# Score products on contiguous key chunks, and values loaded in 256-byte pieces, one pair of heads at a time

## The chip, the cores and the metric

The kernel runs on one NeuronCore of a Trainium2 chip. The metric is the device time of one execution in microseconds (us). The engines are PE (TensorE matmul; PEld is its weight load), DVE (VectorE), ACT (ScalarE), POOL (GpSimd) and SP (SyncE), which here only issues transfers.

## The reference

```python
def rmsnorm(x, g): return x / np.sqrt(np.mean(x * x, -1, keepdims=True) + 1e-06) * g
q_n, k_n = rmsnorm(q, g_q), rmsnorm(k, g_k)
scores = (1 / np.sqrt(64)) * q_n @ k_n.transpose(0, 1, 3, 2)
attn = softmax(scores)                     # over the keys
x = (attn @ v) -> (3584 tokens, 768)       # q, k, v: (8, 12, 448, 64) float32
e = argmax(x @ w_gate + modality_bias[modality_id], 1)      # one of 8 experts
out[t] = gate[t] * relu(x[t] @ w1[e]) @ w2[e]               # w1 768x1024, w2 1024x768
```

Eight batches of twelve heads go through attention over 448 keys of 64 values each; every token of the result then goes through one of eight experts.

## The kernel before, in words

The program has two stages. The first is attention, the second the experts, in blocks of 256 tokens. The change touches the first alone.

**Units and chunks.** Attention goes over 48 units (`NU`); a unit is two heads of one batch. The 2 x 448 keys of a unit are cut into seven chunks of 128, j = 0 to 6. Chunks 0 to 2 hold 384 keys of head 0, chunks 4 to 6 those of head 1, and chunk 3 the 64 keys left of each head. A unit takes seven steps, one a chunk; n = 7 u + j counts them.

**What PE does in a step.** `st` (L844) makes the scores of one chunk, keys on the partitions and 448 queries along the row: one matmul with a high part of the keys (`kkf`, 128 rows, in `w1w`) and one with a low part (`khf`, 65 rows, in `w2ha` or `w1w`). The keys are the stationary operand, so each matmul first loads 128 columns of them. `columns` (L805) says which. In chunk 3 the columns are contiguous, and there are four matmuls, since the heads need one pair each. In the six others the columns lie three apart: chunk j takes every third key from j % 4 on. ACT makes `p`, the exponentials of the scores. `sa` (L812) makes scores once more with queries on the partitions, two units ahead, for the row maxima that DVE takes; its stationary operand is contiguous. Beside these two a step holds at most a few other groups, placed by the numbers of `PLAN` (L34): `tr` (transposing a later unit's normalised keys, step 0, and queries, step 3), `av` (L883, values times `p` of the unit before, steps 1, 4 and 6), `mt` (step 1), `xt` (step 4), `sums` (step 2 of every second unit), `gates` and `recips` (`sp`, step 2 of every fourth unit). So of the six strided chunks five follow such a small group on PE, and chunk 6 follows a `sa`.

**Transfers.** SP issues them in program order. In each unit there are eight `move`s (L764: high and low parts of keys and queries to other partitions, 64 rows of 1,792 bytes), a row of maxima (L839), and the loads of q and k of a later unit (L677). After every third unit comes the store of finished columns (L963) and then `load_v` (L659), which loads the values of three units at once by four transfers. The keys of a chunk lie three apart so that a partition's three values are neighbours in DRAM: `(p j)` gives 768-byte pieces. The order of `move`s matters to PE: those of `tr` of the queries (step 3, at -18) are needed by the first `sa` (at -14) four steps later, those of the keys (at -21) seven steps later.

Of the kernel before, what the change touches and what calls it, by code (L numbers as in the profile page):

```python
# [18 lines left out]
B, H, S, D = 8, 12, 448, 64  # L19
# [3 lines left out]
NP = H // 2  # L23
NU = B * NP
# [42 lines left out]
def kernel(  # L67
# [16 lines left out]
    PE, SY = nc.tensor, nc.sync  # L84
# [52 lines left out]
    def load_gate():  # L137
        with nc.allow_non_contiguous_dma(reason="small gate tables"):
            for half in range(2):
                SY.dma_start(wg[64 * half : 64 * half + 64, :, 8 * half : 8 * half + 8],  # L140
                             w_gate.rearrange("(j h p) e -> h p j e", h=2, p=64)[half])
            SY.dma_start(modr, mod_id.bitcast(I32).rearrange("(b p w) -> p b w", b=B, p=CP))
        SY.dma_start(
            bia.rearrange("p m e -> p (m e)"),
            mod_bias.rearrange("m e -> (m e)").unsqueeze(0).to_broadcast([CP, 2 * NE]),
        )
# [205 lines left out]
    def view(t, off, p, *dims):  # L352
        n = 1
        for d in dims:
            n *= d
        a = t[:p, off : off + n]
        if len(dims) > 1:
            ax = " ".join("abcd"[: len(dims)])
            a = a.rearrange(f"p ({ax}) -> p {ax}", **dict(zip("abcd"[1:], dims[1:])))
        return a  # L360
# [14 lines left out]
    def two(t):  # L375
        return [t[:, 0:S], t[:, S + 64 : WZ]]
# [8 lines left out]
    p_b, v_b = ([view(t, o, 128, *sh) for t in (r2w, at_l)]  # L385
                for o, sh in ((0, (NJ, S)), (PW, (3, NJ, D))))
# [40 lines left out]
    def wload(s, which, halves=(0, 1)):  # L427
        tb, i = tb_of(s)
        raw, src = ((r1, w1v), (r2, w2v))[which]
        for h in halves:  # L430
            G.indirect_dma_start(out=raw[h], out_offset=None, in_=src,
                                 in_offset=IOFF(ap=tb["wi"][:, i, h : h + 1], axis=0),
                                 bounds_check=NE * 256 - 1, oob_is_err=False)
# [212 lines left out]
    if True:  # L646
# [7 lines left out]
        HB = {}  # L654
# [1 line left out]
        X = {}  # L656
        R = {}

        def load_v(hb):  # L659
            b, h0 = hb // 2, 6 * (hb % 2)  # L660
            t = HB.setdefault(hb, {})
            t["v"] = v_b[hb % 2]

            for h in range(2):
                src = v[b, h0 : h0 + 6].rearrange("(u h) s d -> h u s d", h=2)[h]
                SY.dma_start(t["v"][:, :, 4 * h : 4 * h + 3].rearrange("p u j d -> p u (j d)"),
                             src[:, 64 * h : 64 * h + 384].rearrange("u (p j) d -> p u (j d)", j=3))
                SY.dma_start(t["v"][64 * h : 64 * h + 64, :, 3],
                             src[:, 384 * (1 - h) : 384 * (1 - h) + 64].rearrange("u p d -> p u d"))


        def load(u):
            b, h0 = u // NP, 2 * (u % NP)
# [131 lines left out]
        def columns(t, j):  # L805

            if j == 3:
                return [(h, t[:, 384 + 64 * h : 512 + 64 * h]) for h in range(2)]
            h = j // 4
            return [(h, two(t)[h][:, bass.ds(64 * h + j % 4, 128, step=3)])]  # L810

        def sa(u, j):  # L812
            t = T[u]
# [30 lines left out]
        def st(u, j):  # L844
            t = T[u]
            if j == 0:
                t["p"] = p_b[u % 2]
            ps = ps_s.tile([128, 512], F32, tag="s", name=f"st{u}_{j}")
            for first in (True, False):
                for h, l in columns(t["kkf" if first else "khf"], j):  # L850
                    PE.matmul(ps[:, :S], lhsT=l, rhs=t["qq"][:, h] if first else t["ql"][:, h],  # L851
                              start=first and (j != 3 or h == 0), stop=not first and (j != 3 or h == 1))

            def act():
                A.activation(out=t["p"][:, j], in_=ps[:, :S], func=AF.Exp)

            return act
# [310 lines left out]
        for n in range(P["start"], NJ * NU):  # L1168
            i, j = divmod(n, NJ)
# [56 lines left out]
            if 0 <= i < NU and j in CSJ:  # L1226
                h = CSJ.index(j)
# [12 lines left out]
            if done and len(routed) < B - 1 and done[-1] >= (NP * len(routed) + 5) // 4:  # L1240
                b = len(routed)
# [7 lines left out]
                    slow.append(("exp", tables1))  # L1249
            if n == -4:  # L1250
                load_v(0)
                load_gate()
                SY.dma_start(l_d.rearrange("(p r) w -> p (r w)", p=128), zt)
            for h in range(2):
# [10 lines left out]
            if i == NU - 1:  # L1265
                for m in sorted(fin):
                    run(fin, m)
                wload(0, 1)
            if (i + 1) % 3 == 0 and 0 < (i + 1) // 3 < 2 * B:
                load_v((i + 1) // 3)  # L1270

        after = []

# [11 lines left out]
        u, g = NU - 1, NU // 4 - 1  # L1285
# [43 lines left out]
        for s in range(NSTAT):  # L1329
# [34 lines left out]
            for b_ in range(16):  # L1364
                t, j = divmod(b_, 8)
# [79 lines left out]
```

## Time and profile before

| | us |
|---|---|
| median of 3 runs | 1141.43 |
| lowest and highest | 1140.6, 1145.1 |
| the profiled execution | 1139.65 |
| its span, first to last instruction | 1137.9 |
| PE busy | 1089.8 (96%) |
| PE weight loads busy | 856.9 (75%) |
| DVE busy | 863.7 (76%) |
| ACT busy | 827.7 (73%) |
| POOL busy | 656.8 (58%) |

Matmuls are pipelined on PE and their ends are modelled, so its busy time says when it had work, not how fast that went; the distance from the start of one matmul to the start of the next says more. A matmul's weight load can run under the matmul before it.

### The profile page before, as it was taken

The page shows a single profiled execution, that of the slowest core. Times are in us where ns is not written, and L with a number is a line of the kernel's source. Part 1 is how long each engine was busy: PE and PEld are TensorE (multiplying, and loading weights), DVE is VectorE, ACT ScalarE, POOL GpSimd, SP SyncE. Part 2 cuts the span into 40 slices and gives each one's busy share as a digit, 9 for nine tenths or more (in the row PEclk, how much of TensorE's full clock was granted, in tenths as well). Part 3 has the DMA queues.
Part 4 walks back from the last instruction along what each step waited for, and adds up shares of the span by engine and source line. Part 5 has one row for each costly group of instructions (what it writes and reads, how often), then busy time and mean ns, then how long its engine had stood idle before and what let it go on. Part 6 is the DMA issues. An engine that isn't in the chain of part 4 may idle for free. (4 is left out here: it accounts for less than half of the span.)

```text
span 1137.9 us, 19896 instructions
## 1 busy us (share of the span) xinstructions
PE 1089.8 (96%) x6678; PEld 856.9 (75%) x6678; DVE 863.7 (76%) x1598; ACT 827.7 (73%) x1605; POOL 656.8 (58%) x665
## 2 busy tenths in 40 slices
PE   7899999999999999999999999999999999999993
PEld 6655655566565565555568899999999999999981
DVE  4676778988779988789688987767777677776770
ACT  6878888778787787775666677668776687766770
POOL 4577677777777787777764565444244433345430
PEclk8899999999999999999999999999999999999996
DMA  7656567666576666665725111111161111111360
GB/s 170 169 127 154 127 174 173 167 161 148 141 180 162 163 144 160 168 147 114 212 66 189 26 46 59 40 57 56 43 252 41 56 43 56 32 40 56 115 186 11
DMA packets 101345, 131.78 MB, mean 116 GB/s; under 512 B 29979, under 2 KB 95983, under 8 KB 99696
## 3 DMA queue, kind: packets, MB, share of 16 engines
q1 hardware_dynamic: 83588, 88.57, 32.0%
q0 software_dynamic: 17616, 41.80, 11.7%
q8 instruction: 57, 0.93, 0.4%
q14 instruction: 56, 0.46, 0.1%
q10 hardware_dynamic: 28, 0.01, 0.0%
HBM read 148.74 MB, written 22.38 MB: 150 GB/s over the span
## 5 line engine op out<-in xcount | busy, mean ns | idle before, releaser
L485 PE MATMUL ph<-xw,w1w 128*128 128x256 f32 x2016 | 246.1, 283 | 1.8 <-DVE hlw L52 1.0
L485 PEld LDWEIGHTS ph<-xw,w1w 128*128 128x128 f32 x2016 | 243.9, 192 | 3.8 <-issue 1.4
L52 DVE TENSOR_REDUCE at_hlw<-sa 128x1 f32<-128x448 f32 x336 | 206.9, 618 | 48.3 <-PE sa L823 30.0
L52 DVE TENSOR_TENSOR w1w<-r,w1w 128x256 fp32r<-128x256 f32 x360 | 221.0, 672 | 13.8 <-ACT w1w L52 13.5
L52 ACT CAST w1w<-r 128x256 fp32r<-128x256 f32 x360 | 224.8, 722 | 0.0
L851 PE MATMUL st<-w1w 128*128 128x448 f32 (+1 forms) x480 | 191.7, 448 | 1.1 <-ACT r2w L52 0.8
L851 PEld LDWEIGHTS st<-w1w 128*128 128x128 f32 (+1 forms) x480 | 107.3, 239 | 45.1 <-ACT r2w L52 21.2
L52 ACT ACTIVATE hhw<-ph 128x512 fp32r<-128x512 f32 x56 | 33.5, 598 | 121.8 <-PE ph L485 121.8
L52 POOL TENSOR_TENSOR r2w<-r2w 128x448 f32<-128x448 f32 (+1 forms) x72 | 82.4, 1144 | 68.4 <-DVE r2w L52 30.6
L52 ACT ACTIVATE r2w<-st 128x448 f32<-128x448 f32 x168 | 90.0, 541 | 40.7 <-PE st L851 35.7
L823 PE MATMUL sa<-w1w 128*128 128x448 f32 (+1 forms) x288 | 110.6, 385 | 8.9 <-DVE at_hlw L52 5.8
L515 PE MATMUL py<-w2lw,hhw 128*128 128x384 f32 x448 | 113.9, 335 | 0.0
L851 PE MATMUL st<-w1w,w2ha 65*128 65x448 f32 x288 | 102.5, 376 | 3.1 <-DMA r2w<-in_v_dram 2.5
L52 ACT ACTIVATE at_w2lw<-st 128x448 f32<-128x448 f32 x168 | 89.3, 540 | 13.4 <-PE st L851 11.6
L52 POOL TENSOR_TENSOR xrw<-r,at_hlw 112x512 f32<-112x512 f32 x95 | 97.4, 1045 | 2.5 <-PE tr L752 2.2
L52 POOL DMA_INDIRECT out_dram<-yw,lb_oi x22 | 28.3, 1286 | 122.0 <-ACT yw L52 118.9
L515 PEld LDWEIGHTS py<-w2lw,hhw 128*128 128x128 f32 x448 | 80.9, 188 | 0.0
L52 DVE SCALAR_TENSOR_TENSOR hlw<-ph,hhw 128x512 fp32r<-128x512 f32 x56 | 38.7, 691 | 51.9 <-ACT hhw L52 51.9
L52 ACT ACTIVATE w1w<-tr,gs 64x448 fp32r<-64x448 f32 x96 | 60.3, 629 | 23.0 <-DVE xw L52 22.3
L52 POOL TENSOR_TENSOR r2w<-r2w,at_w2lw 64x448 f32<-64x448 f32 (+1 forms) x48 | 54.9, 1144 | 38.0 <-DVE r2w L52 19.5
L851 PEld LDWEIGHTS st<-w1w,w2ha 65*128 65x128 f32 x288 | 70.9, 246 | 5.4 <-DMA r2w<-in_v_dram 2.7
L52 ACT ACTIVATE xrw<-r 112x512 f32<-112x512 f32 (+1 forms) x124 | 64.6, 526 | 9.7 <-DMA r<-in_k_dram 7.2
(297 smaller groups left out, 2297.9 us busy)
## 6 DMA issues: line engine op xcount, KB each, us to landing
w1w<-xw SPq DMA_DIRECT2D x312, 112.0 KB
r<-in_q_dram SPq DMA_DIRECT2D x48, 224.0 KB
r<-in_k_dram SPq DMA_DIRECT2D x48, 224.0 KB
w2ha<-xw SPq DMA_DIRECT2D x72, 112.0 KB
x_d<-at_w2hb SPq DMA_DIRECT2D x8, 672.0 KB
x_d<-yw SPq DMA_DIRECT2D x8, 672.0 KB
r2w<-in_v_dram SPq DMA_DIRECT2D x16, 288.0 KB
at_w2lw<-in_v_dram SPq DMA_DIRECT2D x16, 288.0 KB
```

The lines of the kernel that those rows point to most:

```text
L52: return fn(*a, **kw)
L485: PE.matmul(ps[:, i], lhsT=lt_, rhs=rt_[:, c], start=n == 0, stop=n == 17)
L515: PE.matmul(ps[n][:, :384], lhsT=lt_[:, j, 128 * t : 128 * t + 128], rhs=rt_[:, 384 * n : 384 * n + 384], start=j == 0 and m == 0, stop=j ...
L823: PE.matmul(ps[:, :S], lhsT=t["qq"][r, h, a : a + 128], rhs=t["kk"][h][r], start=True, stop=True)
L851: PE.matmul(ps[:, :S], lhsT=l, rhs=t["qq"][:, h] if first else t["ql"][:, h], start=first and (j != 3 or h == 0), stop=not first and (j != ...
```

## The change

Chunk j of a head now takes 128 neighbouring keys. The values follow: partition p of chunk j holds key 128 j + p, so a piece in DRAM is one key's 64 values, 256 bytes. `load_v` loads one unit instead of three, with four transfers, and is called after every unit up to two before the last, for the unit two later; two calls stand before the first unit.

```diff
-        def load_v(hb):
-            b, h0 = hb // 2, 6 * (hb % 2)
-            t = HB.setdefault(hb, {})
-            t["v"] = v_b[hb % 2]
-
+        def load_v(u):
+            b, h0 = u // NP, 2 * (u % NP)
+            t = HB.setdefault(u // 3, {})
+            t["v"] = v_b[u // 3 % 2]
+            d = t["v"][:, u % 3]
             for h in range(2):
-                src = v[b, h0 : h0 + 6].rearrange("(u h) s d -> h u s d", h=2)[h]
-                SY.dma_start(t["v"][:, :, 4 * h : 4 * h + 3].rearrange("p u j d -> p u (j d)"),
-                             src[:, 64 * h : 64 * h + 384].rearrange("u (p j) d -> p u (j d)", j=3))
-                SY.dma_start(t["v"][64 * h : 64 * h + 64, :, 3],
-                             src[:, 384 * (1 - h) : 384 * (1 - h) + 64].rearrange("u p d -> p u d"))
+                src = v[b, h0 + h]
+                SY.dma_start(d[:, 4 * h : 4 * h + 3],
+                             src[64 * h : 64 * h + 384].rearrange("(j p) d -> p j d", j=3))
+                SY.dma_start(d[64 * h : 64 * h + 64, 3], src[384 * (1 - h) : 384 * (1 - h) + 64])
...
-            return [(h, two(t)[h][:, bass.ds(64 * h + j % 4, 128, step=3)])]
+            return [(h, two(t)[h][:, 64 * h + 128 * (j % 4) :][:, :128])]
...
             if n == -4:
                 load_v(0)
+                load_v(1)
...
-            if (i + 1) % 3 == 0 and 0 < (i + 1) // 3 < 2 * B:
-                load_v((i + 1) // 3)
+            if 0 <= i < NU - 2:
+                load_v(i + 2)
```

PE, DVE, ACT and POOL issue the same work in the same order as before; only SP's queue changes. Here is SP's queue in the middle of attention, across the end of a unit without a store, before. The names are those of the transfers above: `r` takes q and k, `w2ha<-xw` and `w1w<-xw` are moves, the line of 1x7x128 is the row of maxima.

```order
L765 DMA w1w<-xw 64x448 x4
L677 DMA r_0_133<-in_q_dram 112x2x256
L677 DMA r_1_134<-in_k_dram 112x2x256
L765 DMA w2ha<-xw 64x448 x2
L765 DMA w1w<-xw 64x448 x2
L839 DMA w1w<-xw 1x7x128
```

The same place in the changed kernel:

```order
L763 DMA w1w<-xw 64x448 x4
L675 DMA r_0_133<-in_q_dram 112x2x256
L675 DMA r_1_134<-in_k_dram 112x2x256
L666 DMA r2w<-in_v_dram 128x3x64
L668 DMA r2w<-in_v_dram 64x64
L666 DMA r2w<-in_v_dram 128x3x64
L668 DMA r2w<-in_v_dram 64x64
L763 DMA w2ha<-xw 64x448 x2
L763 DMA w1w<-xw 64x448 x2
L837 DMA w1w<-xw 1x7x128
```

Four loads of values now stand ahead of the moves of the next unit's step 0 where none stood. Across the end of a unit with a store the queue was this before:

```order
L963 DMA x_d<-yw 448x1x384
L677 DMA r_0_133<-in_q_dram 112x2x256
L677 DMA r_1_134<-in_k_dram 112x2x256
L666 DMA r2w<-in_v_dram 128x3x192
L668 DMA r2w<-in_v_dram 64x3x64
L666 DMA r2w<-in_v_dram 128x3x192
L668 DMA r2w<-in_v_dram 64x3x64
L765 DMA w2ha<-xw 64x448 x2
```

Here the number of transfers stays, and each of the four carries a third of the bytes. SP issues 537 rows in all where it issued 406 (a row can stand for several equal instructions).

## Rows read from the trace of the kernel before

**Rows 1.** Attention: busy us of PE, PEld, DVE, ACT, POOL; clock, DMA share, GB/s.

```profile
38.00:592.00 554.00, 541.54 (x2781) 323.59 (x2780) 445.77 (x866) 431.86 (x949) 409.54 (x433) 0.98 0.63 154
```

**Rows 2.** Waits of PE from 60 to 590 us: total us, times, longest.

```profile
PE sa L823 <- DVE at_hlw L52: 4.8, 7, 1.5
PE sa L823 <- DMA w1w<-xw: 2.1, 3, 1.1
PE st L851 <- DMA w1w<-xw: 0.6, 2, 0.4
```

**Rows 3.** Timeline of PE: start us, us; a strided chunk behind a `tr`.

```profile
300.60 0.55 PE L752 MATMUL tr<-idn,xrw 112*128 112x112 f32 x4
300.92 0.51 PE L851 MATMUL st<-w1w 128*128 128x448 f32 x1
301.27 0.37 PE L851 MATMUL st<-w1w,w2ha 65*128 65x448 f32 x1
```

**Rows 4.** Timeline of PE: the contiguous chunk 3 behind `sp`, four transposes.

```profile
299.50 0.65 PE L851 MATMUL st<-w1w 128*128 128x448 f32 x2
...
300.40 0.37 PE L818 MATMUL sa<-xw 128*128 128x448 f32 x1
```

**Rows 5.** Timeline of PE: a strided chunk behind an `av`.

```profile
315.78 0.54 PE L851 MATMUL st<-w1w 128*128 128x448 f32 x1
316.15 0.36 PE L851 MATMUL st<-w1w,w2ha 65*128 65x448 f32 x1
```

**Rows 6.** Timeline of PE: the contiguous chunk 3 behind `sums`.

```profile
321.16 0.67 PE L851 MATMUL st<-w1w 128*128 128x448 f32 x2
...
322.07 0.37 PE L818 MATMUL sa<-xw 128*128 128x448 f32 x1
```

**Rows 7.** Timeline of PE: a strided chunk behind a `sa`.

```profile
303.84 0.37 PE L851 MATMUL st<-w1w 128*128 128x448 f32 x1
304.04 0.37 PE L851 MATMUL st<-w1w,w2ha 65*128 65x448 f32 x1
304.25 0.37 PE L823 MATMUL sa<-w1w 128*128 128x448 f32 x1
```

**Rows 8.** Timeline of PE's weight loads: strided keys, then contiguous queries.

```profile
301.06 0.27 PEld L851 LDWEIGHTS st<-w1w,w2ha 65*128 65x128 f32 x1
301.27 0.19 PEld L823 LDWEIGHTS sa<-w1w 128*128 128x128 f32 x1
```

**Rows 9.** Timeline of SP's queue: a unit without store or values.

```profile
301.75 2.42 SPq L765 DMA_DIRECT2D w1w<-xw  x4
304.26 0.55 SPq L677 DMA_DIRECT2D r<-in_q_dram  x1
304.91 0.44 SPq L677 DMA_DIRECT2D r<-in_k_dram  x1
307.91 1.11 SPq L765 DMA_DIRECT2D w2ha<-xw  x2
309.17 1.13 SPq L765 DMA_DIRECT2D w1w<-xw  x2
310.75 0.76 SPq L839 DMA_DIRECT2D w1w<-xw  x1
312.05 2.42 SPq L765 DMA_DIRECT2D w1w<-xw  x4
```

**Rows 10.** Timeline of SP's queue: the end of the next unit, with store and values.

```profile
314.56 0.63 SPq L963 DMA_DIRECT2D x_d<-yw  x1
...
315.96 1.89 SPq L677 DMA_DIRECT2D r<-in_k_dram  x1
317.90 0.53 SPq L666 DMA_DIRECT2D r2w<-in_v_dram  x1
...
320.05 0.63 SPq L668 DMA_DIRECT2D r2w<-in_v_dram  x1
```

**Rows 11.** Timeline of SP's queue: a slow load of values near the end of attention.

```profile
562.64 1.73 SPq L666 DMA_DIRECT2D at_w2lw<-in_v_dram  x1
```

## The prediction

> **What bounds the kernel now.** I read the busy time by stretch first. Attention fills 38 to 592 us, 554 us for 48 units or 11.54 us a unit. In it PE is busy for 541.54 us (98%), DVE for 80%, ACT for 78%, POOL for 74%, and the DMA engines for 63% [rows 1]. Then I read PE's waits in that stretch: twelve of note, seven on DVE (4.8 us in all) and five on moved keys, queries or maxima (2.7 us) [rows 2]. So attention is paced by how fast PE gets through its own queue. The experts' stage is left as it is; whatever attention saves moves it earlier by as much.
>
> Busy time does not show how fast PE goes, so the next view is PE's timeline, read from start to start. Behind a `sa` the two matmuls of a strided chunk start 0.20 us apart, and the next `sa` 0.21 us later [rows 7]. Behind a `tr` the same two start 0.35 us apart, 300.92 to 301.27 [rows 3]; behind an `av` 0.37 us, 315.78 to 316.15 [rows 5]. The reader is to see that nothing was waited for there: the brackets of a wait are missing. What is slow is the weight load of the second matmul. Of the strided keys it took 0.27 us, of contiguous queries right after it 0.19 us [rows 8]. Under a matmul of 448 columns it is hidden; behind a group of small matmuls PE reaches the chunk with no such cover.
>
> Chunk 3 has contiguous columns already and stands behind small groups too, so it prices the change inside this trace. Behind `sp` its four matmuls take 299.50 to 300.40, or 0.90 us [rows 4]. Three of the distances are covered ones of 0.205 us (between the 0.20 and 0.21 of [rows 7]), so the first is 0.90 - 0.615 = 0.285 us, against 0.35 behind a `tr`. Behind `sums` the four take 0.91 us [rows 6], so the first is 0.295 us, against 0.37 behind an `av`.
>
> **The change, part by part.**
>
> *Contiguous keys.* PE's queue is the same instruction for instruction. The steps of a unit put five of the six strided chunks behind a small group, some 240 of 288. Counting them in the timeline with the start-up left out gives 228: 183 behind transposes or tiny matmuls (`tr` 86, `mt` 46, `xt` 41, ten others) and 45 behind products of 448 columns that are narrow in the other direction (`av` 37, `sums` and `gates` 8). The first kind saves 0.35 - 0.285 = 0.065 us each, the second 0.37 - 0.295 = 0.075 us: 183 x 0.065 + 45 x 0.075 = 11.9 + 3.4 = **15.3 us**. The chunks behind a `sa` save nothing. The bounds: none, if the load's time is not due to the step between columns; and 240 x 0.075 = 18 us, if all chunks behave like the second kind.
>
> On this the Trainium skill speaks against the change. Its page "SBUF — State Buffer", section "Door 1: The DMA port swizzle (why `[64,N]` ≈ `[32,N]`)", says that reads run at full rate within a line of 16 bytes, and that fp32 can therefore be strided by up to four elements for free. By that clause a step of three costs nothing, the term above is 0, and the time stays near 1141. The 0.27 against 0.19 us of [rows 8] disagrees with it.
>
> *What the other engines give back.* PE saves 15.3 / 48 = 0.32 us a unit. DVE, ACT and POOL have the same work in a shorter unit; at 80% and below they still fit on average. Where PE waits already, the waited-for work sets the end, and the unit's gain is lost there: 12 waits [rows 2] x 0.32 = 3.8 us. I take this. Its ends are 0, if the waits come no later in a shorter unit, and 9 us, if all 16 units with a store lose theirs too (28 x 0.32).
>
> *SP's queue.* Of a unit without a store SP used 2.42 + 0.55 + 0.44 + 1.11 + 1.13 + 0.76 = 6.41 us of the 10.30 from 301.75 to 312.05 [rows 9], and was idle from 305.35 to 307.91, 2.56 us, just where the new loads go. Four loads of values took 317.90 to 320.68, 2.78 us [rows 10]. So behind them the moves of the keys start about 0.2 us late, or 0.5 us with a shorter unit. What queues behind is those four moves, then the maxima, then the moves of the queries at step 3. The keys are needed seven steps (a unit) after their transposition, so half a microsecond is covered; before the queries' moves, at 312.05, SP had 0.54 us idle after 311.51, which takes up much of the rest. I cost it at nothing. In a unit with a store SP issues as many transfers as before. The store's own price shows there: the load of k behind it took 1.89 us [rows 10] against 0.44 [rows 9]. These units are the late ones today and stay so; the 9 us above is for them. If the cover is gone, the queries' moves come late, and the `sa` of step 0 waits.
>
> *Pieces of 256 bytes.* The values are 48 x 2 x 448 x 64 x 4 bytes = 11.0 MB, of 154 GB/s x 554 us = 85 MB moved in attention [rows 1], so about 13% of a DMA share of 0.63, or 0.08. If a piece of a third the size took as long as a whole one, their share would be 0.24 and the sum 0.79. At the trace's own rate the sum stays 0.63. Either end leaves the engines free time, and the values are loaded a whole unit ahead of the first `av` that reads them. I cost it at nothing. The page "DMA: Bandwidth & Descriptors" of the Trainium skill, section "Specifications", wants at least 512 bytes a transfer for full rate; no row here shows 256-byte pieces by themselves.
>
> *Start-up.* Eight loads stand ahead of the small tables where four stood, some 2.5 us of SP's time, and a third fewer bytes. The moves next in line are needed a unit later. Nothing, within 1 us either way.
>
> *The sum.* 1139.65 (the profiled execution; its span is 1137.9) - 15.3 + 3.8 = 1128.15 us. The median of the runs is 1.8 us above the profiled execution, so I add 1.8: **1130 us**.
>
> **The rivals.**
>
> *A: the gain is given back.* In steps where DVE or SP is behind, PE just waits longer. For it: 80% of DVE's time is busy on average, and PE waits of up to 1.5 us show that it gets behind locally [rows 2]. Against it: twelve waits in 48 units are few. If two thirds of the gain go, 15.3 / 3 = 5.1 us are left: 1139.65 - 5.1 + 1.8 = 1136.
>
> *B: slower, SP's queue becomes the bound.* The place is the run of loads at each unit's end. A load of values late in attention took 1.73 us [rows 11] instead of 0.53 to 0.63 [rows 10]. Per unit SP needs 6.41 us, plus a third of a store and its slow load, (0.63 + 1.89 - 0.44) / 3 = 0.7, plus four loads. That fills today's 11.54 us when a load takes (11.54 - 7.1) / 4 = 1.1 us; above that SP sets the pace and the kernel gets slower. If half of the loads took 1.73 and half 0.6 us, the mean 1.17 gives 7.1 + 4.7 = 11.8 us a unit, 0.25 x 47 = 12 us more: 1153. Against it: at 2.78 us for four, SP is at 9.9 of 11.2 us, and the slow load stands in a stretch where SP was doing little else.
>
> *C: the step is not the cause.* Then the shorter first distance of chunk 3 would have to come from its other operands (its second matmul loads 128 rows instead of 65), or the clause of the page above holds. Time 1141. Against it: [rows 8] compare loads at the same place, and the longer one has fewer rows.
>
> **How the numbers follow.** A measurement of this kernel can tell about 0.5% from no change, 5.7 us, so faster means below 1135.7 and slower above 1147.1. My forecast gets 0.72, from 1121 to 1135: low end 18 us saved and nothing given back, 1139.65 - 18 + 1.8 = 1123, less 2 of the 2.7 us of waits on moved data [rows 2], which smaller loads of values in the units with a store could end; high end 9 given back. A (1136, half a microsecond from the line, counted as the same) gets 0.13, C (1141) 0.07, B (1153) 0.08. So faster 0.72, the same 0.20, slower 0.08. The range has to leave out no more than 0.2: it takes the forecast and A, up to 1139, and leaves out B and C.
>
> **What would show it.** In the changed kernel's timeline a chunk behind a `tr` should start its second matmul 0.28 to 0.29 us after the first, and the weight loads of `st` should take 0.19 us. The mean of a unit should fall from 11.54 to about 11.3 us. SP should show four loads of values in every unit, together below 3 us, and PE's waits on moves should stay below 5 us. The forecast is wrong if the first distances stay at 0.35 us (C), if PE's waits on DVE or moves grow by 10 us (A), or if SP is without a gap from unit to unit and the `sa` of step 0 waits in most units (B).

## The result, and the profile after

| | before | changed |
|---|---|---|
| median of 4 runs, same chip | 1143.26 us | 1131.80 us |
| lowest and highest | 1140.60, 1146.49 | 1130.75, 1132.98 |
| ratio of the medians | | 0.9899 [0.9867, 0.9930] |
| the profiled execution | 1139.65 | 1131.61 |
| its span | 1137.9 | 1129.9 |

In two further comparisons the changed kernel took 1132.00 us (11 runs) beside 1142.59, or 0.9913 [0.9888, 0.9939], and 1131.15 us (6 runs) beside 1141.59, or 0.9902 [0.9873, 0.9931]. It is 10 to 11.5 us faster, and the time is within 2 us of the 1130 that was predicted.

The table by stretch of the changed kernel's attention, 38 us to its last matmuls (us; busy of PE, PEld, DVE, ACT, POOL; clock, DMA share, GB/s; [rows 1] is its fellow):

```profile
38.00:581.00 543.00, 526.48 (x2786) 302.25 (x2784) 441.53 (x867) 429.19 (x949) 412.53 (x433) 0.99 0.67 157
```

Attention takes 543 us where it took 554: 543 / 48 = 11.31 us a unit, as predicted (11.3). PE's busy time fell by 541.54 - 526.48 = 15.1 us, and its idle time grew from 554 - 541.54 = 12.5 to 543 - 526.48 = 16.5 us. Read alone, that is the prediction's 15.3 and 3.8. But a profile is one execution, and its busy time holds the granted clock too: in the profile before, 20 us of attention ran at the lower of TensorE's two levels (1.2 and 2.4 GHz), in this one 14. The experiments take this apart. The experts' stage was not touched. It begins with the first `ph`, at 592.77 us before and 581.54 here, and takes 545.1 and 548.4 us; in the profiles with contiguous keys it lies between 543.9 and 548.4, so I read nothing from those 3 us.

PE's timeline of the changed kernel (start us, us): first a chunk behind an `av`, then one behind a `tr` [rows 5, 3]:

```profile
308.99 0.47 PE L849 MATMUL st<-w1w 128*128 128x448 f32 x1
309.30 0.37 PE L849 MATMUL st<-w1w,w2ha 65*128 65x448 f32 x1
...
309.71 0.55 PE L750 MATMUL tr<-idn,xrw 112*128 112x112 f32 x4
310.03 0.45 PE L849 MATMUL st<-w1w 128*128 128x448 f32 x1
310.32 0.37 PE L849 MATMUL st<-w1w,w2ha 65*128 65x448 f32 x1
```

The second matmul starts 310.32 - 310.03 = 0.29 us after the first where it was 0.35, and 0.31 behind the `av` where it was 0.37. The whole stage bears it out: the medians of this distance fell from 350 to 287 ns behind `tr`, 354 to 290 behind `mt`, 349 to 290 behind `xt`, 375 to 311 behind `av`. The 27 units that have neither a wait nor the lower clock in either profile take 0.31 us less on average, which would be 48 x 0.31 = 14.9 us. The weight loads of the keys are as short as forecast; that of the last matmul above:

```profile
310.12 0.19 PEld L849 LDWEIGHTS st<-w1w,w2ha 65*128 65x128 f32 x1
```

PE's waits from 60 to 590 us in the changed kernel (total us, times, longest), beside [rows 2]:

```profile
PE sa L821 <- DVE at_hlw L52: 4.3, 4, 1.5
PE sa L821 <- DMA w1w<-xw: 3.4, 5, 1.0
PE st L849 <- DMA w1w<-xw: 1.2, 2, 1.0
```

Waits on DVE are what they were; those on moves, maxima among them, grew from 2.7 to 4.6 us, under the 5 us foreseen. SP's queue in the changed kernel, a unit without a store (start us, us):

```profile
297.57 0.45 SPq L666 DMA_DIRECT2D r2w<-in_v_dram  x1
298.07 0.50 SPq L668 DMA_DIRECT2D r2w<-in_v_dram  x1
298.62 0.59 SPq L666 DMA_DIRECT2D r2w<-in_v_dram  x1
299.25 0.50 SPq L668 DMA_DIRECT2D r2w<-in_v_dram  x1
299.91 1.13 SPq L763 DMA_DIRECT2D w2ha<-xw  x2
```

Four loads take 297.57 to 299.75, or 2.2 us, and the keys' moves follow 0.16 us later. SP's gap before these moves, 2.56 us in [rows 9], is gone, and nothing waits for that here.

### The profile page after: what moved, and what is told of

Its sections match the earlier page's. It is cut to its first block, busy times and chain, and to the rows that moved or that the text cites. A ratio compares the mean times of both kernels' runs of the same rounds, so it can differ in the third digit from the quotient of the medians.

```text
span 1129.9 us, 20043 instructions
## 1 busy us (share of the span) xinstructions
PE 1076.3 (95%) x6678; PEld 837.3 (74%) x6678; DVE 859.6 (76%) x1598; ACT 824.8 (73%) x1605; POOL 662.7 (59%) x665
## 2 busy tenths in 40 slices
DMA packets 127970, 131.79 MB, mean 117 GB/s; under 512 B 68891, under 2 KB 122607, under 8 KB 126320
## 5 line engine op out<-in xcount | busy, mean ns | idle before, releaser
L849 PE MATMUL st<-w1w 128*128 128x448 f32 (+1 forms) x480 | 177.1, 418 | 3.8 <-ACT r2w L52 3.5
L849 PEld LDWEIGHTS st<-w1w 128*128 128x128 f32 (+1 forms) x480 | 85.6, 192 | 48.2 <-ACT r2w L52 21.5
L52 POOL TENSOR_TENSOR r2w<-r2w 128x448 f32<-128x448 f32 (+1 forms) x72 | 83.4, 1158 | 55.4 <-DVE r2w L52 17.9
L821 PEld LDWEIGHTS sa<-w1w 128*128 128x128 f32 (+1 forms) x288 | 55.4, 192 | 22.5 <-DVE at_hlw L52 10.2
```

The lines of the kernel that those rows point to most:

```text
L52: return fn(*a, **kw)
L821: PE.matmul(ps[:, :S], lhsT=t["qq"][r, h, a : a + 128], rhs=t["kk"][h][r], start=True, stop=True)
```

## The experiments

All were run beside the kernel before on the same chip (runs in brackets, 95% intervals behind the ratios):

| kernel | us | before | ratio |
|---|---|---|---|
| keys contiguous, old loads | 1136.91 (12) | 1140.85 (23) | 0.9968 [0.9947, 0.9990] |
| old keys, new loads | 1136.64 (12) | 1140.85 (23) | 0.9966 [0.9948, 0.9983] |
| old keys, new loads, another chip | 1137.86 (12) | 1141.59 (17) | 0.9964 [0.9944, 0.9984] |
| changed, that second chip | 1131.15 (6) | 1141.59 (17) | 0.9902 [0.9873, 0.9931] |
| changed, a third chip | 1132.00 (11) | 1142.59 (20) | 0.9913 [0.9888, 0.9939] |
| keys contiguous, old loads moved | 1132.60 (10) | 1142.59 (20) | 0.9918 [0.9893, 0.9943] |
| old keys, old loads moved | 1138.89 (12) | 1143.97 (17) | 0.9953 [0.9926, 0.9980] |
| changed, no loads behind the store | 1129.31 (6) | 1140.85 (23) | 0.9909 [0.9889, 0.9930] |
| changed, 768-byte pieces | 1130.53 (6) | 1142.59 (20) | 0.9888 [0.9857, 0.9919] |
| changed, every load twice | 1218.60 (4) | 1142.59 (20) | 1.0682 [1.0637, 1.0728] |
| changed, twelve loads behind the store | 1218.34 (6) | 1143.97 (17) | 1.0654 [1.0609, 1.0699] |

### Is it the step between columns?

The kernel before, with chunk 1 at step 2, chunk 4 at step 1 and the others at step 3.

```diff
-            return [(h, two(t)[h][:, bass.ds(64 * h + j % 4, 128, step=3)])]
+            s = {0: 3, 1: 2, 2: 3, 4: 1, 5: 3, 6: 3}[j]
+            return [(h, two(t)[h][:, bass.ds(0, 128, step=s)])]
```

> One look at prices, on the kernel before: chunk 1 (behind the tr of the keys) takes columns two apart, chunk 4 (behind the tr of the queries) contiguous ones, the others keep three; the scores then use wrong keys, so the output is not the reference's. Theory L (reads run at full rate while at least two values come from one line of 16 bytes): step two costs as step one, a first distance of 0.29 us and a weight load of 0.19 us behind both tr, step three 0.35 and 0.27. Theory S (any step but one is slow): step two 0.35 and 0.25 or more. Theory P (the load grows with the bytes it spans): step two half-way, 0.31 to 0.33 us, weight load 0.22 to 0.24. Time 1132 to 1140 by all.

PE's timeline of it (start us, us); in the order of time the chunks have step 2, 3 and 1:

```profile
328.82 0.55 PE L752 MATMUL tr<-idn,xrw 112*128 112x112 f32 x4
329.14 0.46 PE L852 MATMUL st<-w1w 128*128 128x448 f32 x1
329.43 0.36 PE L852 MATMUL st<-w1w,w2ha 65*128 65x448 f32 x1
...
331.62 0.51 PE L852 MATMUL st<-w1w 128*128 128x448 f32 x1
331.97 0.37 PE L852 MATMUL st<-w1w,w2ha 65*128 65x448 f32 x1
...
333.41 0.55 PE L752 MATMUL tr<-idn,xrw 112*128 112x112 f32 x4
333.73 0.45 PE L852 MATMUL st<-w1w 128*128 128x448 f32 x1
334.02 0.37 PE L852 MATMUL st<-w1w,w2ha 65*128 65x448 f32 x1
```

The weight loads of the three second matmuls, in the same order:

```profile
329.23 0.20 PEld L852 LDWEIGHTS st<-w1w,w2ha 65*128 65x128 f32 x1
...
331.76 0.27 PEld L852 LDWEIGHTS st<-w1w,w2ha 65*128 65x128 f32 x1
...
333.81 0.19 PEld L852 LDWEIGHTS st<-w1w,w2ha 65*128 65x128 f32 x1
```

Steps 1 and 2 load in 0.19 and 0.20 us and start the second matmul 0.29 us after the first, behind a `tr` as in [rows 3], where it is 0.35. Step 3, here behind `mt`, loads in 0.27 us and starts it after 0.35. Over the whole stage the medians of this distance are 289, 294 and 351 ns for chunks 4, 1 and 2 (steps 1, 2 and 3), those of the load 192, 201 and 265 ns. The step is the cause, and a step of two costs next to nothing. The one run took 1139.67 us.

### Each part alone

The keys alone are the kernel before with one line changed.

```diff
-            return [(h, two(t)[h][:, bass.ds(64 * h + j % 4, 128, step=3)])]
+            return [(h, two(t)[h][:, 64 * h + 128 * (j % 4) :][:, :128])]
```

> Only the key columns are made contiguous; the values load as before, 768-byte pieces for three units at a time, so the values no longer meet their keys and the output is not the reference's (same instructions, same sizes). My theory (the weight load of keys three apart is the whole gain, and the loads of values in every unit cost a little on SP): the first distance of a chunk behind a tr falls to 0.29 us as in the changed kernel, PE's waits on moved data stay near the 2.7 us of the kernel before, and the time is 1128 to 1131 us, 1 to 3 us below the changed kernel's 1131.8. Rival 1 (the gain comes from spreading the loads of values evenly): 1141 to 1145. Rival 2 (loads of values are free): 1131 to 1133, as the changed kernel.

The new loads alone are the changed kernel with the old line for the keys and, in `load_v`, pieces that go with it:

```diff
-            return [(h, two(t)[h][:, 64 * h + 128 * (j % 4) :][:, :128])]
+            return [(h, two(t)[h][:, bass.ds(64 * h + j % 4, 128, step=3)])]
...
-                             src[64 * h : 64 * h + 384].rearrange("(j p) d -> p j d", j=3))
+                             src[64 * h : 64 * h + 384].rearrange("(p j) d -> p j d", j=3))
```

> Only the loads of values change: unit by unit, two units ahead, four transfers a unit, still in 768-byte pieces; keys stay three apart. My theory: 0 to 4 us slower than the kernel before (1143.3), 1143 to 1147 us, with PE's waits on moved data at 4 to 8 us instead of 2.7 between 60 and 590 us, and first distances at 0.35 us. Rival 1 (spreading the loads is what gains): 1132 to 1137. Rival 3 (SP is the bound): over 1150.

Both expectations missed. The keys alone gave 4 us where 10 to 13 were expected; the loads, expected to cost up to 4 us, gave 4. PE's waits from 60 to 590 us with the keys alone:

```profile
PE st L851 <- DMA w1w<-xw: 5.2, 4, 2.4
PE sa L823 <- DVE at_hlw L52: 4.3, 4, 1.5
PE sa L823 <- DMA w1w<-xw: 1.8, 3, 1.0
```

The first line stands out: `st` waits 5.2 us, where the kernel before waits 0.6 [rows 2]. By the semaphores that its weight loads wait for, it is each time the row of maxima that is late: it goes into the second matmul of `st`, and SP issues it behind the moves of the keys. How the longest of these waits comes about is seen in four views of this kernel. SP's queue from a store at 410.43 us on:

```profile
410.43 0.64 SPq L963 DMA_DIRECT2D x_d<-at_w2hb  x1
...
411.83 1.85 SPq L677 DMA_DIRECT2D r<-in_k_dram  x1
413.74 0.54 SPq L666 DMA_DIRECT2D at_w2lw<-in_v_dram  x1
...
415.69 0.62 SPq L668 DMA_DIRECT2D at_w2lw<-in_v_dram  x1
416.41 2.80 SPq L765 DMA_DIRECT2D w2ha<-xw  x2
...
420.67 0.81 SPq L839 DMA_DIRECT2D w1w<-xw  x1
```

The last row is the row of maxima. The row of 2.80 us is long because of a wait between its two moves; of SP's waits from 411 to 421 us (total us, times, longest) it is this one:

```profile
SPq L765 <- DMA x_d<-at_w2hb: 1.6, 1, 1.6
```

PE's timeline, the wait in brackets:

```profile
422.38 0.48 PE L851 MATMUL st<-w1w 128*128 128x448 f32 x1
425.24 0.74 PE L851 MATMUL st<-w1w,w2ha 65*128 65x448 f32 x1 [2.39 <-DMA w1w<-xw]
```

The table by stretch around it:

```profile
419.00:422.00 3.00, 3.00 (x22) 1.56 (x20) 2.61 (x6) 2.81 (x8) 2.11 (x2) 1.00 1.14 276
422.00:425.00 3.00, 0.85 (x9) 0.19 (x1) 0.51 (x1) 0.69 (x2) 1.11 (x2) 0.98 0.85 198
425.00:427.00 2.00, 1.76 (x7) 1.62 (x8) 0.61 (x1) 0.93 (x2) 1.92 (x2) 0.50 0.81 232
427.00:430.00 3.00, 3.00 (x10) 1.36 (x11) 1.82 (x4) 2.57 (x5) 0.19 (x1) 0.50 0.45 88
```

The first move of the keys is issued 416.41 - 410.43 = 6.0 us after the store, behind a slow load of k and 672 KB of values. The second waits until the store has landed. In these traces SP's transfers take eight semaphores in turn, and each waits for the landing of the transfer eight places before it; with four loads behind the store, that is the store for the second move. The DMA engines are full from 419 to 422 us (a share of 1.14). So the row of maxima is issued 10.2 us after the store and lands at 425.19, and PE goes on at 425.24, 2.4 us late. Then a second loss comes: after PE's pause the granted clock stands at 0.50, the 1.2 GHz level, from 425 to past 430 us, and the matmuls there start 0.37 to 0.54 us apart, not 0.2.

A shorter wait can do the same. In the kernel before, PE's timeline:

```profile
292.71 0.64 PE L823 MATMUL sa<-w1w 128*128 128x448 f32 x1 [1.11 <-DMA w1w<-xw]
```

and the table by stretch right behind:

```profile
292.80:296.00 3.20, 3.20 (x12) 1.98 (x14) 1.82 (x4) 1.66 (x3) 2.22 (x3) 0.50 0.56 154
```

After a wait of 1.07 us at 382.60 us in the same profile the clock stayed at 1.00. How long attention runs at the lower level so differs between executions of one kernel: 14, 20 and 14 us in three profiles of the changed one.

That second loss is in the times too. Over the 77 runs of the kernel before on four chips, a mean granted clock that is 0.001 lower goes with 1.0 us more (correlation -0.72). An estimate from the two levels agrees: 2 us at half the clock take 0.0009 off the mean of 1138 us, and cost 1 us where PE is the limit. These runs average 0.980, the keys alone 0.978, the new loads alone 0.982 and 0.982. So some 2 us of what the keys lose, and as much of what the loads gain, goes with the clock. This is a correlation; no run held the clock fixed.

To see whether the parts add up, the changed kernel and the new loads alone were run once more on one chip.

> The changed kernel once more, on the same chip as the kernel with the old keys and the new loads below, so that what the keys are worth beside the new loads is read from one chip. Theory S (the two parts add up): with the old loads the keys alone gave 0.9968, so they give about 0.997 here too, 3 to 5 us less than the kernel below. Theory T (late moves behind three units' values hid part of the keys' gain; the new loads let it through): 7 to 11 us less than the kernel below, a quotient of 0.990 to 0.994. Against the kernel before: 0.989 to 0.992 by either.

> Keys three columns apart as before, values loaded unit by unit as in the changed kernel, in 768-byte pieces. 0.9966 of the kernel before was measured on another chip; the same is expected, 0.995 to 0.998. By theory S the changed kernel is 3 to 5 us below this one, by theory T 7 to 11 us.

The changed kernel took 1131.15 us and the loads alone 1137.86: beside the new loads the keys are worth 6.7 us (some 4 to 10 by the spread of the runs), a quotient of 0.9941. That is between the theories and nearer to T. Beside the old loads they were worth 3.9 us (1 to 6). Whether the two really differ stays open. Either is far from 15.

Where the rest went is told by the profiles, those of the next section among them. Attention is taken here from the first `st` to the first `ph`; the times at 1.2 GHz are summed from each trace's record of the clock, and the last column is an estimate that takes half of them off:

| attention, us | time | PE idle | at 1.2 GHz | time less half of that |
|---|---|---|---|---|
| before | 555.1 | 12.5 | 20 | 545 |
| loads alone | 550.1 | 11.6 | 14 | 543 |
| loads alone, second chip | 550.9 | 13.4 | 10 | 546 |
| old keys, old loads moved | 554.0 | 14.1 | 17 | 545 |
| keys alone | 549.6 | 17.9 | 27 | 536 |
| keys contiguous, old loads moved | 540.1 | 15.7 | 7 | 537 |
| changed | 543.3 | 16.5 | 14 | 536 |
| changed, second chip | 547.2 | 17.6 | 20 | 537 |
| changed, third chip | 542.9 | 15.1 | 14 | 536 |

The keys add 2 to 5 us of idle time, about what the prediction gave back. With the clock taken off, they are worth some 8 us in attention wherever the loads stand. No profile shows a gain by the loads there beyond the clock; one profile a kernel can't tell 1 or 2 us.

### Where the old loads stand

The next kernels keep the old loads of three units and call them after the first unit of three, away from the store. The first of them has the contiguous keys, the other the old ones.

```diff
-            if (i + 1) % 3 == 0 and 0 < (i + 1) // 3 < 2 * B:
-                load_v((i + 1) // 3)
+            if i >= 0 and i % 3 == 0 and i // 3 + 1 < 2 * B:
+                load_v(i // 3 + 1)
```

> Contiguous keys with the old loads of values (three units at once, 768-byte pieces, four transfers), but issued after the first unit of three instead of the third, so never behind a store; as with keys alone the values don't meet their keys and the output is not the reference's. Theory W (what keys alone lost, 0.9968 where PE's part promises 0.987, was lost in units where the store and the three units' values stand in the queues together and the moves behind them land late): 0.989 to 0.991 of the kernel before. Theory B (three units' values at once are what delays, wherever they stand): 0.996 to 0.998, as with keys alone.

> The kernel before (keys three apart, values of three units at once, 768-byte pieces, four transfers), with one edit: the loads of values are issued after the first unit of three instead of the third, so not behind the store. Theory W (the loads behind the store cost the kernel before some 4 us, and that is what the new loads alone won): 0.995 to 0.998 of the kernel before, as e2 did, with the moves behind a store issued 3.4 us after it instead of 6.0. Theory U (loading unit by unit is what won in e2): 0.999 to 1.002.

Both did as theory W says: 0.9918 and 0.9953. With the same bytes, in the same pieces, by the same number of transfers, moving one call is worth 5 us (2 to 8 by the interval of the second). In SP's queue of the first the keys' move behind a store is issued 3.5 us after it:

```profile
406.65 0.63 SPq L963 DMA_DIRECT2D x_d<-at_w2hb  x1
...
408.05 1.82 SPq L677 DMA_DIRECT2D r<-in_k_dram  x1
410.12 1.11 SPq L765 DMA_DIRECT2D w2ha<-xw  x2
```

PE's largest waits of that kernel from 60 to 590 us, in which `st` waits for no transfer any more:

```profile
PE sa L823 <- DVE at_hlw L52: 5.7, 8, 1.5
PE sa L823 <- DMA w1w<-xw: 1.9, 3, 1.1
```

This profile is the fastest of its ten runs, 1125.3 us.

The changed kernel gets the same in another way. Its four loads stay behind the store, so its move starts 5.7 us after it, nearly as with the keys alone (6.0); but they carry a third of the bytes, and it has landed 8.6 us after the store, not 10.3, and the row of maxima 10.5 us, not 11.6 (with the moved call, 7.9 and 8.7; medians over the stores, by the semaphores in the traces). In the 8 us from 4 us after a store on, the DMA engines are busy for 0.85 with the keys alone and for 0.72 in the changed kernel (means over six stores each). For one and the same store, the keys alone:

```profile
313.93:321.93 8.00, 8.00 (x46) 4.28 (x42) 6.38 (x12) 6.02 (x14) 5.54 (x6) 1.00 0.82 217
```

And the changed kernel:

```profile
311.86:319.86 8.00, 8.00 (x46) 4.28 (x42) 6.38 (x12) 6.02 (x14) 5.55 (x6) 1.00 0.73 180
```

PE's waits on moves, maxima among them, go with it: 7.0 us with the keys alone, 1.9 with the moved call, 3.3 to 4.7 in the three profiles of the changed kernel. With the old keys they do not. The move lands earlier there as well (10.4 us after the store before, 7.8 with the moved call, 8.8 with the new loads), but the waits are 2.7, 3.1, and 2.1 and 3.4 us. So beside the old keys the gain of the loads is shown, and some 2 us of it go with the clock; how the rest comes about is not shown.

If that is what counts, a kernel with contiguous keys and 256-byte pieces whose loads all stand away from the store (chunk by chunk for three units, one head after the first unit and one after the second) should gain once more. Against the kernel before, beside the line for the keys:

```diff
-        def load_v(hb):
+        def load_v(hb, heads=(0, 1)):
...
-            for h in range(2):
+            for h in heads:
...
-                SY.dma_start(t["v"][:, :, 4 * h : 4 * h + 3].rearrange("p u j d -> p u (j d)"),
-                             src[:, 64 * h : 64 * h + 384].rearrange("u (p j) d -> p u (j d)", j=3))
+                for j in range(3):
+                    a = 64 * h + 128 * j
+                    SY.dma_start(t["v"][:, :, 4 * h + j], src[:, a : a + 128].rearrange("u p d -> p u d"))
...
-            if (i + 1) % 3 == 0 and 0 < (i + 1) // 3 < 2 * B:
-                load_v((i + 1) // 3)
+            if i >= 0 and i % 3 < 2 and i // 3 + 1 < 2 * B:
+                load_v(i // 3 + 1, (i % 3,))
```

> The changed kernel's contiguous keys and 256-byte pieces, but the loads of values go three units at a time again, one transfer a chunk (eight for three units instead of twelve), four after the first and four after the second unit of three, none in the units with a store. Same result as the reference. My theory (what the change gives back beside DVE's waits is SP being late in the units with a store): PE's waits on moved data fall from 4.6 us between 60 and 590 us to under 2, and the time is 1127 to 1130 us, 2 to 4 us below the changed kernel. Rival 2 (the loads of values cost nothing): 1131 to 1133, the same as the changed kernel.

1129.31 us is in the range given, but the kernel before was at its fastest on that chip too, and the ratio, 0.9909, is the changed kernel's (0.9899 to 0.9913). No gain over the change is shown. PE's waits on moves fell to 3.0 us, not under 2, and PE's idle time in attention, 17.4 us, is within the 15.1 to 17.6 of the changed kernel's profiles: what the moves no longer cost, PE waits for elsewhere.

### Pieces of 256 bytes

The changed kernel with the old pieces:

```diff
-                             src[64 * h : 64 * h + 384].rearrange("(j p) d -> p j d", j=3))
+                             src[64 * h : 64 * h + 384].rearrange("(p j) d -> p j d", j=3))
```

> The changed kernel with 768-byte pieces instead of 256-byte ones, everything else the same (unit by unit, four transfers a unit); the values don't meet their keys, so the output is not the reference's. My theory (piece size costs nothing, the DMA engines have room): 0.989 to 0.991 of the kernel before, the same as the changed kernel. Rival (small pieces cost): 0.984 to 0.987.

0.9888 with 768-byte and 0.9899 to 0.9913 with 256-byte pieces, within each other's intervals (on one chip, 1130.53 and 1132.00 us; a cost of up to some 4 us is not excluded), though the page of the profile counts 103,394 DMA packets with the one and 127,970 with the other.

### SP's queue

Every load of values twice, the second time into a spare tile:

```diff
+        vd = cp.tile([128, 7, 64], F32, name="vd")
...
-            d = t["v"][:, u % 3]
-            for h in range(2):
+            v_ = t["v"][:, u % 3]
+            for d, h in ((v_, 0), (v_, 1), (vd, 0), (vd, 1)):
```

> The changed kernel with every load of values issued twice, the second into a spare tile that nobody reads (eight transfers a unit instead of four). Theory Q (SP has room for four loads a unit and not for eight: it needs 7.1 us a unit without them, and 8 x 0.65 = 5.2 more make 12.3, over the 11.3 us of a unit): SP sets the pace and the time rises by (12.3 - 11.3) x 46 = 46 us, to 1170 to 1185 us. Theory R (SP is far from a bound, transfers are issued in gaps): 1132 to 1140.

And the twelve loads of three units in one go, behind the store:

```diff
                 load_v(1)
+                load_v(2)
...
-            if 0 <= i < NU - 2:
-                load_v(i + 2)
+            if i >= 0 and i % 3 == 2:
+                for u in range(i + 1, min(i + 4, NU)):
+                    load_v(u)
```

> The changed kernel's keys, pieces and transfers, but the twelve loads of three units all issued after the third unit, behind the store. Theory W (the moves queued behind store and loads are what makes PE wait, and twelve issues of some 0.6 us put them 4.8 us later than four did): slower than keys alone (0.997), at 1.005 to 1.02 of the kernel before, PE's waits on moved data at 15 to 30 us. Theory V (position does not matter, the count of transfers does): 0.990 to 0.993, as the changed kernel.

Both went the way that was expected and much further, 76 and 74 us slower. PE's largest wait from 60 to 650 us with eight loads a unit:

```profile
PE st L851 <- DMA w1w<-xw: 31.5, 21, 5.7
```

With twelve loads behind the store:

```profile
PE st L849 <- DMA w1w<-xw: 47.6, 14, 7.3
```

It is the same wait for the row of maxima as above, only longer. With eight loads SP is nearly full, as theory Q says: from 60 us to the end of attention its issues, with the pauses of up to 0.2 us between them, fill 559 of 609 us (92%), where they fill 447 of 519 (86%) in the changed kernel. The 40 us between 559 and 519 are near the 46 of theory Q; the rest comes on top. A part of it is seen in one of the gaps that are left (start us, us):

```profile
314.08 0.54 SPq L668 DMA_DIRECT2D at_w2lw<-in_v_dram  x1
...
318.23 0.50 SPq L670 DMA_DIRECT2D vd<-in_v_dram  x1
321.73 1.14 SPq L765 DMA_DIRECT2D w2ha<-xw  x2
```

Eight loads took 4.7 us, and then SP was idle for 3.0 us. SP's only wait from 318 to 322 us says for what:

```profile
SPq L765 <- DMA at_w2lw<-in_v_dram: 2.9, 1, 2.9
```

The move waits for the landing of the transfer eight places before it, which is now the first load, the one issued at 314.08 behind the store. So large transfers delay a move by more than the time of issuing them. With twelve loads behind the store SP fills only 441 of 606 us (73%); there it is the place of the loads, not SP's total. And the pauses cost twice here as well. With twelve loads, in the table by stretch around one of these waits:

```profile
324.00:327.00 3.00, 0.52 (x1) 0.29 (x1) 0.00 (x0) 0.00 (x0) 2.44 (x3) 0.50 0.57 126
327.00:330.00 3.00, 2.84 (x11) 1.93 (x12) 1.08 (x2) 2.04 (x4) 2.13 (x3) 0.50 0.75 137
```

PE pauses for 4.8 us and comes back to a granted clock of 0.50 until about 330 us. In attention PE is idle for 69 and 68 us and runs at 1.2 GHz for 85 and 96 us with eight and with twelve loads, against 17 and 14 us in the changed kernel. The mean clock of the two profiled executions is 0.957 and 0.946, against 0.982 for the changed kernel.

## Why the prediction was right, and where it was wrong

**What bounds the kernel: right.** Attention is PE's queue, and the gain came there, in the first distance behind small groups.

**Contiguous keys, 15.3 us: right** as a saving on PE's path, and a little large. The first distances fell by 0.06 us each, some 14 us in all, and a unit without a wait by 0.31 us. The 0.075 us of the second kind was too much: behind `sums` the contiguous chunk's first distance has a median of 0.31 us, not 0.295.

**What the other engines give back, 3.8 us: near in size, wrong in kind, and not the whole.** PE's idle time grew by 4.0 us from the profile before to the changed one, and by 5.4, 4.2 and 1.6 us in the other pairs that differ in the keys. The step that failed is "12 waits x 0.32": it lets the waits that are there already grow, seven of them on DVE, and those did not (4.8 us before, 4.3 changed and with the keys alone). Waits on moves and maxima grew, to 4.6 us and with the keys alone to 7.0, and behind waits PE goes on at half its clock, which the sum had no term for. In the runs the keys brought 3.9 us beside the old loads and 6.7 beside the new, not 15.3 - 3.8 = 11.5. At an equal mean clock, taking 1.0 us for 0.001, it would be 6 to 8 us. The 1.3 us by which the distances were priced too high, and 2 to 4 us that no run accounts for, make up the rest.

**SP's queue, "I cost it at nothing": wrong.** Its issuing was priced well (9.9 of 11.2 us a unit, and 86% measured). But the new loads are worth about 4 us, as a gain. I wrote that the units with a store "are the late ones today and stay so", since SP issues as many transfers there as before. What is late is the landing of the moves and, with the keys alone, above all of the row of maxima behind them; with a third of the values' bytes ahead, the keys' moves land 8.6 us after the store, not 10.3, and the maxima after 10.5, not 11.6. With contiguous keys PE's waits on moves fall with it; some 2 of the 4 us go with the clock; beside the old keys the cause of the rest stays open. I did see the chance, as up to 2 us at the low end of the range.

So the sum had 11.5 us for the keys and nothing for the loads. On one chip the loads brought 3.7 us and the keys, beside them, 6.7. The total is right because two errors of 4 to 5 us cancel; that part is luck.

**Pieces of 256 bytes at nothing: right**, as far as the intervals tell. The DMA share of attention was 0.65 with 768-byte and 0.67 with 256-byte pieces, and no time followed from it. The Trainium skill ("DMA: Bandwidth & Descriptors", section "Specifications") wants at least 512 bytes for full rate; no run here shows a loss by it. (Chunk 3's values came in pieces of 256 bytes before, too.)

**Rival A (given back, 1136)** is where the keys alone came out (1136.91 us), by waits on moves and by the clock more than by DVE; the loads made up for it. **Rival B (SP's queue)** does not happen at four loads a unit and does at eight. Its price left something out: I let SP become full by slow issues, and a move also waits for the transfer eight places before it to land.

**Rival C (not the step)** fell. On this the Trainium skill ("SBUF — State Buffer", section "Door 1: The DMA port swizzle (why `[64,N]` ≈ `[32,N]`)") has two clauses. That fp32 can be strided by four elements for free disagrees with the trace: step 3 loads in 0.27 us and step 1 in 0.19. That full bandwidth needs at least two reads in each 16-byte line agrees with the trace: step 2, at 0.20 us, has two values in a line, and step 3 often one.

## What to carry to other kernels

A stationary operand with fp32 columns three apart cost nothing here under a matmul of 448 columns and 0.06 us behind a group of small ones; look for it in the distance from start to start, and in the weight load's own row. When a faster engine is the whole gain, ask what its shorter round meets: here over half of it went back, in part into idle time and a lower clock after waits. Before two profiles are set against each other, compare how long each ran at the lower clock: in the nine above it was 7 to 27 us of attention. Where a small transfer that PE needs stands in a queue behind a large one that nobody needs soon, move the large one: one moved call was worth 5 us here, half as much as the whole change.

## What the runs showed of the hardware that was not expected

- A pause of PE can cost more than its length. After waits of 1.1, 2.4 and 4.8 us the granted clock read 0.50 (the 1.2 GHz level) for 3 us of matmuls and more; after another wait of 1.1 us it stayed at 1.00. Over 77 runs of one kernel, 0.001 of mean clock went with 1.0 us.
- A step of two fp32 columns loads as fast as contiguous ones (0.20 and 0.19 us for 128 columns), a step of three takes 0.27.
- SP's transfers wait in these traces for the landing of the transfer eight places before. Four more loads of values a unit, 4.7 us of issuing in place of 2.2, filled SP's queue to 92%, made a move wait 2.9 us for a load to land, and the kernel 6.8% slower.
